# Re-spacing the substitution columns, the shared sums and the masks of a DeltaNet and hard-swish MLP kernel

## The chip, the cores and the metric

The kernel runs on one core of one Trainium2 chip. Its time is the device time of one execution in microseconds (us). Engines are named as in the profile: PE is TensorE (PEld its weight loads), DVE is VectorE, ACT is ScalarE, POOL is GpSimd, SP is SyncE. L756 is line 756 of the kernel before; in the kernel after, lines behind the first hunk stand one or two lower.

## The reference

A linear-attention recurrence (DeltaNet, with 4 batches, 8 heads, 768 tokens, head size 48) is followed by an MLP with a hard-swish (3072 tokens, 384 to 2048 to 384). All is fp32.

```python
k_n = k / (norm(k) + 1e-06)
for t in range(768):                     # state: (B, H, 48, 48)
    y[:, :, t] = einsum('bhd,bhde->bhe', q[:, :, t], state)
    v_old = einsum('bhde,bhd->bhe', state, kt)
    state = state + bt * einsum('bhd,bhe->bhde', kt, vt - v_old)
x = y.transpose(0, 2, 1, 3).reshape(3072, 384)
h = x @ w_in
out = (h * clip(h + 3, 0, 6) / 6) @ w_out
```

## The kernel before

**Chunks.** The recurrence is done in 24 chunks t of 32 tokens of all four batches (128 rows). Within a chunk the dependence of tokens on each other is a triangular system with a 32x32 matrix L for each batch and head. Its inverse X is found first, and then the chunk costs a few small matmuls. The names that matter:

- `prep(t)`: normalises k into `kb` (POOL, L502), makes the masks `mb` from beta (POOL, two operations of 128x256, L478), transposes k and q on PE (`pt`, L518), copies them to `KQ` (ACT), forms the scores `sc` (PE, L539) and multiplies them by `mb` into `L` and `LB` (DVE, L550), and at the end makes `bkb` (POOL, L490). `mb` has a single buffer, so a mask waits until L550 of the chunk before has read the last one.
- `inverse(g)`: the forward substitution for a group g of four chunks, 128 systems at once, on DVE: a transpose of L in (L461), 30 columns with two operations each (L751 multiplies into `pr`, L756 subtracts it from `A`; together 60 steps), a memset of the diagonal (L760) and a transpose out into `X` (L465). All four chunks of group g need this X. Groups 3 to 6 hold chunks 9 to 12, 13 to 16, 17 to 20 and 21 to 23.
- `chain(t)`: what goes from chunk to chunk. PE forms `ks` from the state (L798). DVE makes R in two halves: R1 is L892 (two operations), R2 is L898 (one). PE forms `pz` from X and R (L819), ACT copies it out, PE forms the state's update `su` (L927), and DVE subtracts it from `state` (L945). On its side the output: y from `ks` (ACT L835, DVE L811), plus `py` (PE L819, DVE L854, called y2 below), transposed on PE (`yt`, L864) into `xT` for the MLP.

**MLP.** Blocks of two chunks. `up` multiplies by w_in, `down` by w_out. From block 2 on `down_by_seven` does the down product as a 2x2 block scheme of seven products, with sums of g on DVE (L1197) and of the outputs on POOL and DVE (L1221). From block 5 on `up_by_eleven` does the up product in eleven block products for every pair of feature tiles j (0 to 7): `begin(j)` runs four matmuls, ACT copies the four quarters to `g` (L1069), POOL makes three sums of 128x128 that two products share (`plus_minus`, L1020), `end(j)` runs seven more matmuls into the same PSUM tile, and DVE adds the shared sums to it (L1085, L1086). The hard-swish follows on ACT (L1092, L1096) and DVE (L1099).

**Order.** The whole program is recorded by hand: each engine executes its instructions in the order in which the Python code emits them. The first chunks follow a written list (`ORDER`). From chunk 5 on, a loop emits every chunk as 15 units u = 0 to 14. In each unit it first takes the steps of chain and prep that `plan` sets for this u, then one unit of the MLP (one piece of `up`, `down` or their block forms, some 1.7 us of PE), then some steps of `fill`, which is the inverse of the next group for most of the time. For a chunk with i = t's place in its group: `ks` is emitted in u 0, R1 in u 1, R2 in u 2, `pz` in u 4, L550 in u 5, the update and y2 in u 8 to 10. The inverse of the next group is opened in u 6 of i = 1 (L461; for group 3 it is u 0 of i = 2). `left` counts the 62 takes that remain. In a unit

```python
room = max(1.65 - USED[mode["of"]] - CHAIN.get(u, 0), 0.15) / mode["mean"]
due += room * left / max((GS - i) * NU - u, 1)
due = min(due, 3.0)
take(fill, int(due))
left, due = max(left - int(due), 0), due - int(due)
```

`USED` is what DVE has to do for the MLP in such a unit, `CHAIN` what the chain asks of it in unit u, `mean` a mean of the room. In i = 0 two steps a unit are taken, and at u 2 of i = 0 `drain(fill)` emits all that is left, since `pz` in u 4 needs X. The drain stands behind R2 in that unit. Line `if i == 1 == ready[0] and 5 < u < 9: continue` leaves out the first units after the opening.

Of the kernel before, what the change touches and what calls it, by code (L numbers as in the profile page):

```python
# [15 lines left out]
ALU = mybir.AluOpType  # L16
# [30 lines left out]
def kernel(  # L47
# [21 lines left out]
    nc = tc.nc  # L69
# [3 lines left out]
    P = B * C  # L73
# [131 lines left out]
    for j, value in enumerate((1.0, -1.0)):  # L205
        m = mask2[:, j, :]
        for b in range(B):
            nc.gpsimd.memset(mask2[rows(b), j, :], value)
            nc.gpsimd.affine_select(
                out=mask2[rows(b), j, :], in_=mask2[rows(b), j, :], pattern=[[1, C]],  # L210
# [286 lines left out]
    def prep(t, whole=True):  # L497

        g, i = group(t)
        kb, qb = kbufs[t % NKB], qbufs[t % NQB]  # L500
        needs(*([("bkb", t - NKB)] if t >= NKB else []), *(pad(t) if t < NKB and t else []))
        nc.gpsimd.tensor_tensor(  # L502
            out=kb[:, :, 0:D], in0=kfs[g][:, i],
            in1=invs.pop(t).unsqueeze(2).to_broadcast([P, H, D]), op=ALU.mult,
        )
        past.add(("kb", t))
        if whole:
            drain(mask(t))
        yield

        for j, src in enumerate((kb, qb)):
            if j == 1:
                needs(("q", t))
                past.add(("qT", t))
            ring("pm", NPM, ("pt", t, j))
            pt = psM.tile([128, NP, P], FP32, name="pt", tag="pm")
            for p in range(NP):
                nc.tensor.transpose(  # L518
                    pt[:, p, :], src[:, 2 * p : 2 * p + 2].rearrange("p e w -> p (e w)"), ident[:]
                )  # L520
            yield 1
            if j == 0:
                ring("KQ", NKQ, ("KQ", t))
                KQ = work.tile([128, NP * B // 2, 4, C], FP32, name="KQ", bufs=NKQ)
            read(("pt", t, j))
            nc.scalar.activation(
                out=KQ[:, :, 0:4:3, :] if j == 0 else KQ[:, :, 1:3, :],
                in_=pt[:].rearrange("q p (x y c) -> q (p x) y c", y=2, c=C), func=ACTF.Copy,
            )
            yield  # L530
        ring("pc", NPC, ("sc", t))
        sc = psC.tile([P, 2, 512], FP32, name="sc", tag="pc")
        scv = sc[:, :, 0 : NP * 2 * C].rearrange("p e (a j w) -> p e a j w", a=NP, j=2)
        for p in range(NP):
            for b in range(B):
                for e in range(2):
                    r = slice(DP * e, DP * e + DP)
                    kq = KQ[r, p * B // 2 + b // 2]
                    nc.tensor.matmul(  # L539
                        scv[rows(b), e, p],  # L540
                        lhsT=kq[:, 3 if b % 2 else 0, :],
                        rhs=kq[:, 3:1:-1, :] if b % 2 else kq[:, 0:2, :],
                        start=True, stop=True,
                    )
        yield
        needs(*([("BZ", t - NLB)] if t >= NLB else []))
        LB = work.tile([P, H, C], FP32, name="LB", bufs=NLB)
        mb = mbs.pop(t)
        for j, out in enumerate((lowers(t), LB)):
            nc.vector.tensor_tensor(  # L550
                out=out.rearrange("p (e a) w -> p e a w", e=2), in0=scv[:, :, :, j, :],
                in1=mb[:, :, :, j, :], op=ALU.mult,
            )
        past.add(("L", t))
        KQs[t], LBs[t] = KQ, LB
        read(("sc", t), *([("KQ", 0)] if t == 0 else []))
        if whole:
            drain(scaled(t))
        yield
# [396 lines left out]
    mode = {"of": "down", "mean": 0.72}  # L956
# [51 lines left out]
    UF = 5  # L1008
# [10 lines left out]
    def plus_minus(out, a, b, op):  # L1019
        nc.gpsimd.tensor_tensor(out=out, in0=a, in1=b, op=op)  # L1020
# [28 lines left out]
    def up_by_eleven(blk):  # L1049
        needs(("sums", blk))  # L1050
        B11, T3x, B21, B22, B31, B32 = x_tiles(blk)
        phs, ready = {}, {}

        def mm(ph, n, w, x, start=False, stop=False):
            nc.tensor.matmul(  # L1055
                ph[:, n], lhsT=w, rhs=x, start=start, stop=stop, skip_group_check=True
            )

        def begin(j):
            key = ("ph", blk, "by", j)  # L1060
            ring("pm", NPM, key)
            ph = phs[j] = psM.tile([128, 4, P], FP32, name="ph", tag="pm")
            mm(ph, 0, W11[:, j], B11, start=True)
            mm(ph, 1, S1[:, j], T1x)
            mm(ph, 2, W21[:, j], T3x)
            mm(ph, 3, S2[:, j], T2x)
            gs[blk, j] = mlp.tile([128, 2, TB], FP32, name="g", bufs=NFC // 2)
            gt = gs[blk, j][:].rearrange("p i (t c) -> p (i t) c", c=P)
            nc.scalar.activation(out=gt, in_=ph[:], func=ACTF.Copy)  # L1069
            plus_minus(gt[:, 1], gt[:, 1], gt[:, 2], ALU.add)  # L1070
            plus_minus(gt[:, 2], gt[:, 0], gt[:, 1], ALU.add)
            plus_minus(gt[:, 0], gt[:, 0], gt[:, 3], ALU.add)

        def end(j):
            ph = phs.pop(j)
            mm(ph, 0, W12[:, j], B21)
            mm(ph, 1, S4[:, j], B22)
            mm(ph, 2, W22[:, j], T4x)
            mm(ph, 0, W13[:, j], B31)
            mm(ph, 1, W13[:, j], B32)  # L1080
            mm(ph, 2, W23[:, j], B31)
            mm(ph, 3, W23[:, j], B32, stop=True)
            g = gs[blk, j][:].rearrange("p i c -> p (i c)")
            gt = gs[blk, j][:].rearrange("p i (t c) -> p (i t) c", c=P)
            nc.vector.tensor_tensor(out=gt[:, 3], in0=ph[:, 3], in1=gt[:, 2], op=ALU.add)  # L1085
            nc.vector.tensor_tensor(  # L1086
                out=gt[:, 1:3], in0=ph[:, 1:3],
                in1=gt[:, 0].unsqueeze(1).to_broadcast([128, 2, P]), op=ALU.add,
            )

            def first():
                nc.scalar.activation(out=gt[:, 0], in_=ph[:, 0], func=ACTF.Copy)  # L1092
                read(("ph", blk, "by", j))
                ro = mlp.tile([128, CB, DM], FP32, name="o", bufs=1)
                r = ro[:].rearrange("p c m -> p (c m)")[:, 0 : 2 * TB]
                nc.scalar.activation(out=r, in_=g, func=ACTF.Relu, bias=half, scale=1.0 / 6.0)  # L1096

                def rest():
                    nc.vector.scalar_tensor_tensor(  # L1099
                        out=g, in0=r, scalar=1.0, in1=g, op0=ALU.min, op1=ALU.mult  # L1100
                    )

                ready[j] = rest

            ready[j] = first
            if j == NPR - 1:
                past.add(("up", blk))

        def go(j):
            if j in ready:  # L1110
                ready.pop(j)()

        begin(0)
        yield
        begin(1)
        yield
        for j in range(NPR):
            end(j)
            go(j - 1)
            if j + 2 < NPR:  # L1120
                yield
                begin(j + 2)
                go(j)
                yield
            else:
                go(j)
                if j == NPR - 1:
                    go(j)
                yield
# [148 lines left out]
    def mlp_units():  # L1278
# [20 lines left out]

        for blk in range(1, N // CB):  # L1300
            mode["of"] = "down"
            mode["mean"] = 0.72 if blk + 1 < UF else 0.45
            sums = weight_sums() if blk == UF - 1 else iter(())
            for _ in downs(blk):
                next(sums, None)
                next(sums, None)
                yield
            if blk + 1 < N // CB:
                mode["of"] = "eleven" if blk + 1 >= UF else "up"
                for n, _ in enumerate((up_by_eleven if blk + 1 >= UF else up)(blk + 1)):  # L1310
                    if blk + 1 == FIRST and n >= HF:
                        drain(rest)
                        if n % 2:
                            last_quarter(n - HF - 1)
                    yield
# [11 lines left out]
    def drain(gen):  # L1327
        for _ in gen:
            pass
# [87 lines left out]
    with tc.manual_schedule():  # L1417
# [11 lines left out]
        loads = iter(())  # L1429
        left = due = 0  # L1430
        USED = {"up": 0.42, "eleven": 1.0, "down": 0.8}
        CHAIN = {1: 0.75, 2: 0.75, 3: 0.4, 4: 0.4, 6: 0.8, 9: 0.8, 10: 0.8}
        for t in range(LS, N):
            g, i = group(t)
            ch = chain_of(t)
# [29 lines left out]
            for u in range(NU):  # L1465
# [15 lines left out]
                settle(1)  # L1481
                while evicts:
                    evicts.pop(0)()
                if i == 1 == ready[0] and 5 < u < 9:
                    continue
                if i == 0 or not left:
                    take(fill, 2 if i or u < 2 else u > 4)
                    continue
                room = max(1.65 - USED[mode["of"]] - CHAIN.get(u, 0), 0.15) / mode["mean"]
                due += room * left / max((GS - i) * NU - u, 1)  # L1490
                due = min(due, 3.0)
                take(fill, int(due))
                left, due = max(left - int(due), 0), due - int(due)
            drain(ch)
# [32 lines left out]
```

## Time and profile before

| | us |
|---|---|
| median of 3 runs | 680.05 |
| the three runs | 678.49, 680.05, 1275.28 |
| profiled execution | 677.9 |
| its span, first to last instruction | 676.2 |
| busy in it: PE / PEld / DVE / ACT / POOL | 638.2 / 579.8 / 500.0 / 272.3 / 221.1 |

The profiled execution's own time is 1.7 us longer than its span. In the profile's line of 40 slices, one slice is 16.9 us. Chunk 5, where the loop starts, begins at 160.5 us (its `ks`), and the last chunk (23) at 615.0 us, so a chunk is some 25 us long. A line of a group of instructions reads: source line, engine, operation, output and inputs, shape, count, then busy time and mean duration, then the idle time of the engine just before them and what ended it.

### The profile page before, as it was taken

The numbers are of one execution on the slowest core, as the hardware profiler recorded it, in microseconds if no ns is written. First come the engines' busy times: TensorE is split into PE (matmuls) and PEld (weight loads), VectorE is DVE, ScalarE is ACT, GpSimd is POOL, SyncE is SP. The second block draws the span as 40 slices with busy tenths as digits, with TensorE's granted clock in tenths as the row PEclk, the third lists the DMA queues.
The fourth block names the chain that finished last, engine by engine and source line by source line (L and its number), as shares of the span: only waits on it lengthen the run. The fifth ranks groups of instructions, "written<-read, shape, count | busy, mean of one in ns | idle before, by whom it ended". The sixth has DMA issues, their size and how long they took to land.

```text
span 676.2 us, 26940 instructions
## 1 busy us (share of the span) xinstructions
PE 638.2 (94%) x11768; PEld 579.8 (86%) x11768; DVE 500.0 (74%) x1226; ACT 272.3 (40%) x532; POOL 221.1 (33%) x376
## 2 busy tenths in 40 slices
PE   2568989999999999999999999999999999999997
PEld 2457977776689988988999999999999999999997
DVE  5998867888546699747888957998747998557264
ACT  5995767422143132232244244244244143143250
POOL 6230232002521121236165255065052151442340
PEclk9978989999999999999999999999999999999999
DMA  7896435402041030032030030020020020010000
GB/s 190 214 231 147 97 75 147 82 1 48 17 87 22 3 71 3 2 72 37 3 71 4 3 73 2 3 61 2 3 49 3 2 49 2 15 25 3 26 1 23
DMA packets 88501, 33.29 MB, mean 49 GB/s; under 512 B 80160, under 2 KB 83232, under 8 KB 88384
## 3 DMA queue, kind: packets, MB, share of 16 engines
q1 hardware_dynamic: 88128, 31.29, 20.4%
q8 instruction: 92, 1.51, 0.9%
q10 hardware_dynamic: 256, 0.30, 0.2%
q14 instruction: 25, 0.20, 0.1%
HBM read 26.84 MB, written 4.72 MB: 47 GB/s over the span
## 4 chain that ended last, share of the span: by engine, by line
PE 82%; DMA 6%; DVE 6%; issue 2%; ACT 1%; SPq 1%; POOL 1%; DVEq 0%; ACTq 0%; POOLq 0%
PE po L1211 27%; PE ph L1055 17%; PE ph L983 15%; PE po L1146 6%; PE ks L798 3%; DMA w_out<-in_moe_w_in_dram 3%; PE py L819 3%; PE pz L819 3%; PE su L927 3%; PE pt L518 2%; PE sc L539 2%; DMA qb<-in_q_dram 1%; PE yt L864 1%; DVE A L756 1%; DVE pr L751 1%
## 5 line engine op out<-in xcount | busy, mean ns | idle before, releaser
L1055 PE MATMUL ph<-xT,w_in 128*128 128x128 f32 x784 | 122.9, 278 | 0.0
L983 PE MATMUL ph<-xT,w_in 128*128 128x256 f32 (+1 forms) x576 | 117.0, 356 | 0.7 <-ACT spare L348 0.5
L1211 PE MATMUL po<-w_out,g 128*128 128x192 f32 x640 | 110.6, 326 | 0.0
L983 PEld LDWEIGHTS ph<-xT,w_in 128*128 128x128 f32 x576 | 96.3, 197 | 12.6 <-DVE g L994 0.6
L1055 PEld LDWEIGHTS ph<-xT,w_in 128*128 128x128 f32 x784 | 103.9, 192 | 1.3
L1020 POOL TENSOR_TENSOR g<-g 128x128 f32<-128x128 f32 x168 | 79.7, 476 | 75.4 <-ACT g L1069 66.2
L1211 PEld LDWEIGHTS po<-w_out,g 128*128 128x128 f32 x640 | 104.1, 190 | 0.2
L1211 PE MATMUL po<-spare,g 128*128 128x192 f32 x480 | 86.7, 332 | 0.0
L1211 PEld LDWEIGHTS po<-spare,g 128*128 128x128 f32 x480 | 77.2, 190 | 1.8
L1221 POOL TENSOR_TENSOR o<-o,u 128x192 f32<-128x192 f32 x18 | 18.6, 1035 | 167.2 <-ACT o L1218 93.5
L991 ACT ACTIVATE g<-ph,halves 128x256 f32<-128x256 f32 (+1 forms) x96 | 41.2, 437 | 78.3 <-PE ph L983 78.1
L1069 ACT ACTIVATE g<-ph 128x512 f32<-128x512 f32 x56 | 33.4, 597 | 80.5 <-PE ph L1055 77.0
L1197 DVE TENSOR_TENSOR g<-g 128x256 f32<-128x256 f32 x160 | 62.7, 440 | 3.5 <-PE po L1211 3.1
L756 DVE TENSOR_TENSOR A<-A,pr 128x30 f32<-128x30 f32 (+9 forms) x150 | 59.5, 397 | 3.6
L751 DVE TENSOR_TENSOR pr<-A 128x30 f32<-128x30 f32 (+9 forms) x150 | 56.1, 374 | 3.4
L994 DVE SCALAR_TENSOR_TENSOR g<-g,ph 128x256 f32<-128x256 f32 (+1 forms) x96 | 35.0, 371 | 25.2 <-ACT g L991 24.7
L348 ACT ACTIVATE spare<-spare,places 128x768 uint16<-128x768 uint16 (+1 forms) x56 | 52.5, 941 | 1.6 <-DMA spare<-in_moe_w_in_dram 0.6
L1099 DVE SCALAR_TENSOR_TENSOR g<-o,g 128x512 f32<-128x512 f32 x56 | 42.5, 759 | 6.6 <-ACT o L1096 6.6
L1218 ACT ACTIVATE o<-po 128x192 f32<-128x192 f32 x40 | 13.3, 331 | 80.5 <-PE po L1211 76.3
L1146 PE MATMUL po<-w_out,g 128*128 128x384 f32 x128 | 45.6, 493 | 0.0
L1096 ACT ACTIVATE o<-g,halves 128x512 f32<-128x512 f32 x56 | 40.5, 722 | 12.6 <-DVE g L1099 8.9
L478 POOL TENSOR_TENSOR mb<-beta_tok,mask 128x256 f32<-128x256 f32 x38 | 27.0, 730 | 55.8 <-DVE LB L550 55.8
(141 smaller groups left out, 985.2 us busy)
## 6 DMA issues: line engine op xcount, KB each, us to landing
kf<-in_k_dram SPq DMA_DIRECT2D x96, 48.0 KB, 2.8
qb<-in_q_dram SPq DMA_DIRECT2D x96, 48.0 KB, 2.8
vf<-in_v_dram SPq DMA_DIRECT2D x96, 48.0 KB, 2.1
out_dram<-o SPq DMA_DIRECT2D x92, 48.0 KB, 1.6
spare<-in_moe_w_in_dram SPq DMA_DIRECT2D x4, 768.0 KB, 7.7
w_out<-in_moe_w_in_dram SPq DMA_DIRECT2D x4, 768.0 KB, 8.0
w_out<-in_moe_w_out_dram SPq DMA_DIRECT2D x4, 768.0 KB, 5.6
spare<-in_moe_w_out_dram SPq DMA_DIRECT2D x4, 768.0 KB, 4.4
```

The lines of the kernel that those rows point to most:

```text
L348: nc.scalar.activation(out=z, in_=z if n else d.bitcast(I16)[:, :, :, 3], func=func, bias=places[:, n : n + 1], scale=scale,)
L751: nc.vector.tensor_tensor(out=pv, in0=A[:, j + 1 :, j].unsqueeze(2).to_broadcast([n, w, j]), in1=A[:, j, 0:j].unsqueeze(1).to_broadcast([n ...
L756: nc.vector.tensor_tensor(out=A[:, j + 1 :, 0:j], in0=A[:, j + 1 :, 0:j], in1=pv, op=ALU.subtract)
L819: nc.tensor.matmul(ps[rows(place(b)), D * h : D * h + D], lhsT=m(h)[rows(b)], rhs=z[rows(b), D * at(h) : D * at(h) + D], start=True, stop= ...
L983: nc.tensor.matmul(ph[:, cols], lhsT=w_in[:, s, f * 128 : (f + 1) * 128], rhs=xT[:, s, cols], start=(s == 0), stop=(s == NKT - 1),)
L991: nc.scalar.activation(out=g, in_=ph, func=ACTF.Relu, bias=half, scale=1.0 / 6.0)
L1020: nc.gpsimd.tensor_tensor(out=out, in0=a, in1=b, op=op)
L1055: nc.tensor.matmul(ph[:, n], lhsT=w, rhs=x, start=start, stop=stop, skip_group_check=True)
L1099: nc.vector.scalar_tensor_tensor(out=g, in0=r, scalar=1.0, in1=g, op0=ALU.min, op1=ALU.mult)
L1146: nc.tensor.matmul(pos[c][:], lhsT=gs[blk, f // 2][:, f % 2, c * P : (c + 1) * P], rhs=w_out[:, f, :], start=(f == 0), stop=(f == NFC - 1),)
L1197: nc.vector.tensor_tensor(out=A(f, *out), in0=A(f, *a), in1=A(f, *b), op=op)
L1211: nc.tensor.matmul(ps[n][:], lhsT=A(f - f % 2, *a)[:, f % 2], rhs=b[:, f], start=(f == 0), stop=(f == HF - 1),)
```

## The change

Five edits.

1. In `prep`, the mask is emitted one step later: not directly after `kb` but after the first transposes and their copy.
2. In `up_by_eleven`, the three shared sums become two POOL operations. The first takes both 128x128 sums in one operation whose first and output operands run over the quarters backwards (`3:1:-1`), and what the two DVE operations of `end` add is renamed to match; the larger one (two quarters) now stands first.
3. Columns start in u 7 of i = 1 instead of u 9 (`5 < u < 7`).
4. `due` is held at 2.6, so at most two steps a unit are taken instead of three.
5. `CHAIN` gets entries for u 0 and u 14 and smaller ones for u 6 and u 10; `mean` for blocks from 4 on is 0.4 instead of 0.45.

```diff
@@ prep
         past.add(("kb", t))
-        if whole:
-            drain(mask(t))
         yield
...
                 in_=pt[:].rearrange("q p (x y c) -> q (p x) y c", y=2, c=C), func=ACTF.Copy,
             )
+            if whole and j == 0:
+                drain(mask(t))
             yield
@@ up_by_eleven, begin
-            plus_minus(gt[:, 1], gt[:, 1], gt[:, 2], ALU.add)
-            plus_minus(gt[:, 2], gt[:, 0], gt[:, 1], ALU.add)
-            plus_minus(gt[:, 0], gt[:, 0], gt[:, 3], ALU.add)
+            plus_minus(gt[:, 3:1:-1], gt[:, 0:2], gt[:, 3:1:-1], ALU.add)
+            plus_minus(gt[:, 0], gt[:, 0], gt[:, 2], ALU.add)
@@ up_by_eleven, end
-            nc.vector.tensor_tensor(out=gt[:, 3], in0=ph[:, 3], in1=gt[:, 2], op=ALU.add)
             nc.vector.tensor_tensor(
                 out=gt[:, 1:3], in0=ph[:, 1:3],
-                in1=gt[:, 0].unsqueeze(1).to_broadcast([128, 2, P]), op=ALU.add,
+                in1=gt[:, 3].unsqueeze(1).to_broadcast([128, 2, P]), op=ALU.add,
             )
+            nc.vector.tensor_tensor(out=gt[:, 3], in0=ph[:, 3], in1=gt[:, 0], op=ALU.add)
@@ mlp_units
-            mode["mean"] = 0.72 if blk + 1 < UF else 0.45
+            mode["mean"] = 0.72 if blk + 1 < UF else 0.4
@@ the loop
-        CHAIN = {1: 0.75, 2: 0.75, 3: 0.4, 4: 0.4, 6: 0.8, 9: 0.8, 10: 0.8}
+        CHAIN = {0: 0.45, 1: 0.75, 2: 0.75, 3: 0.4, 4: 0.4, 6: 0.5, 9: 0.8, 10: 0.6, 14: 0.2}
...
-                if i == 1 == ready[0] and 5 < u < 9:
+                if i == 1 == ready[0] and 5 < u < 7:
                     continue
...
-                due = min(due, 3.0)
+                due = min(due, 2.6)
```

## The prediction, made before the changed kernel ran

> **What bounds the kernel now.** I read the page's engine lines and slices first, then the waits of PE from 200 us on, then a table of windows cut at the `ks` of the chunks, then timelines of DVE and PE at the places that had lost time.
>
> ```profile
> span 676.2 us, 26940 instructions
> PE 638.2 (94%) x11768; PEld 579.8 (86%) x11768; DVE 500.0 (74%) x1226; ACT 272.3 (40%) x532; POOL 221.1 (33%) x376
> PE   2568989999999999999999999999999999999997
> PEld 2457977776689988988999999999999999999997
> PEclk9978989999999999999999999999999999999999
> ...
> PE pz L819 <- DVE R L898: 1.8, 3, 0.8
> PE py L819 <- issue: 0.5, 1, 0.5
> PE pz L819 <- ACT o L1218: 0.4, 1, 0.4
> PE yt L864 <- DVE y L854: 0.4, 1, 0.4
> PE ph L983 <- DVE g L994: 0.2, 1, 0.2
> ```
>
> PE is full from the ninth slice on, at full clock. The five waits are all that it had from 200 us to the end: 3.3 us. The rest of its 38 us of idle time is in the opening, which `ORDER` writes, and at the very end; no edit reaches either. The windows of chunks 8, 12, 15, 16 and 20 (length, PE, PEld, DVE, ACT, POOL busy) say where:
>
> ```profile
> 240.90:267.10 26.20, 25.97 (x426) 22.02 (x425) 24.78 (x70) 9.14 (x19) 2.77 (x4) 1.00 0.19 36
> 343.40:369.50 26.10, 25.40 (x495) 24.44 (x495) 22.97 (x52) 12.47 (x25) 16.84 (x30) 1.00 0.20 41
> 419.70:445.40 25.70, 25.26 (x459) 24.15 (x458) 23.57 (x66) 6.50 (x14) 5.42 (x9) 1.00 0.04 10
> 445.40:471.90 26.50, 25.30 (x495) 24.37 (x495) 24.27 (x53) 12.56 (x25) 16.97 (x30) 1.00 0.17 33
> 544.00:568.20 24.20, 23.37 (x424) 22.73 (x422) 21.42 (x54) 12.09 (x25) 10.37 (x22) 1.00 0.13 28
> ```
>
> Length less PE: 0.23, 0.70, 0.44, 1.20 and 0.83 us, 3.4 in all; DVE is over 88% busy in each. Chunk 16 shows how it comes about (four lines of DVE's timeline, then one of PE's; start, duration, engine, line):
>
> ```profile
> 449.81 0.53 DVE L756 TENSOR_TENSOR A<-A,pr 128x220 f32<-128x220 f32 x1
> 450.37 0.52 DVE L751 TENSOR_TENSOR pr<-A 128x210 f32<-128x210 f32 x1
> 450.81 0.73 DVE L892 SCALAR_TENSOR_TENSOR R<-ks,parity,vf 128x192 f32<-128x192 f32 x2
> ...
> 452.89 0.60 DVE L898 SCALAR_TENSOR_TENSOR R<-ks,parity,R 128x384 f32<-128x384 f32 x1
> 453.64 0.88 PE L819 MATMUL pz<-R,X 32*32 32x48 f32 x64 [0.83 <-DVE R L898]
> ```
>
> Columns stand without a gap ahead of R1; R2 ends at 453.49 and `pz` starts 0.15 us later, after 0.83 us of idle PE. So PE sets the time and DVE's lateness at R2 is the only thing to win.
>
> **What the Trainium skill says.** "Perfetto Trace Analysis", Identifying the Most-Contended Engine: matmul busy time misleads, the weight loads' share is the better sign. The trace agrees with PE as bound: PEld is 22.7 to 24.4 us in the last four windows. "SBUF — State Buffer", Who interferes with whom: a DVE operation with two SBUF inputs and a GpSimd one that reads SBUF exclude each other. The trace fits: the subtraction of 128x108 took 0.27 us at 423.13, with POOL idle, and 0.68 at 367.62, while POOL made a mask. "GPSIMD Engine Reference", Elementwise — side-by-side cycle accounting: a fixed part plus 2.6 cycles an element at 1.2 GHz, 2.2 ns. Here 128 elements took 476 ns (168 of L1020) and 256 took 728 (L1020 on w_in): 1.97 ns an element, 224 ns fixed. Performance pitfalls for Q7 kernels, in the same page: an inner step over 8 bytes costs half as much again. Here only the outer step is reversed and the inner stays 4 bytes, so I charge nothing.
>
> **The change part by part.** I counted the DVE instructions in the built order of both kernels. PE, ACT and SP have the same instructions in the same order; only DVE's and POOL's orders differ. So PE's work is unchanged and the sum is over waits.
>
> *Columns, gains.* Steps ahead of R2, counted from the last point at which DVE had been idle, before and after:
> - Chunk 8: 16 to 12. At 0.40 us a step R2 and the L994 behind R1 come 1.6 us sooner; the 0.23 goes.
> - Chunk 12: 12 to 9, at 0.5: 1.5 us sooner; 0.2 goes. The other 0.5 in this chunk is the wait in `py` for "issue", which nothing here touches: it stays.
> - Chunk 15: 12 to 8, the four smallest (0.21 to 0.27): 0.96 us sooner; 0.44 goes.
> - Chunks 16 and 20: 12 to 9 each, at 0.53: 1.6 us sooner against 0.83 lost; both go.
> - Chunk 16, `yt` behind y2 (0.37): eight steps to seven larger ones since DVE's last idle point at 458, 3.28 to about 3.0 us: 0.3 goes.
>
> Sum 0.23 + 0.2 + 0.44 + 0.83 + 0.83 + 0.3 = 2.8 us.
>
> *Columns, losses.* With two a unit the substitution ends later.
> - Chunk 9: all 60 steps and the transpose stood ahead of R1. Now two steps stand in each of u 0 and u 1 and the drain behind R2 holds six steps, the memset and the transpose. R2 then ends near 271.7. Six small steps (1.45 us from start to start, as at 265 to 266.7), 0.12 and 1.98 give X at 275.2, so `pz`, which ran at 274.77, starts at 275.3: 0.6 us lost. If POOL ran beside them (0.3 more a step) it would be 2.4 more; POOL then waited for ACT until 275.3, so I take 0.6.
> - Chunks 13, 17 and 21: memset and transpose move to u 0, still ahead of R1. Two, three and three more steps stand behind the last L1099 (0.55 to 0.85 us) and one fewer ahead of it (0.6). Chunk 13: 0; chunk 17: 0.2; chunk 21 has 0.8 us of slack between R2 and `pz`: 0.
> - Chunk 14: four small steps, 0.94 us, now stand ahead of y2, whose slack to `yt` is 0.97: 0, with no cover left; chunks 10 and 18 have 2.0 and 1.5.
>
> Sum 0.8.
>
> *Two operations for three.* 3 x 476 = 1.43 us becomes 728 + 476 = 1.20, 56 times: 13 us less POOL. POOL is idle 75 us ahead of L1020, so that is hidden; DVE's wait for POOL (14.7 us, seven waits) shortens, but those lie where R2 has slack. Bounds: if the reversed operand cost as two, nothing is won; if it cost twice 728, a j takes 1.9 us of the 3.4 that its two units last, still hidden. I take 0.
>
> *Masks.* A mask waits less at the head of POOL's queue (32.3 us in three waits), with the weight sums of block 4 and other sums behind it. It is needed at L550, three or four units (5 to 7 us) after its new place and lasts 1.2 to 1.7 us. Hidden; 0 either way, to 0.5 lost if a mask fell behind a waiting L1221.
>
> Total: -2.8 + 0.8 = -2.0 us. The profiled execution would go from 677.9 (span 676.2 and 1.7 around it) to 675.9. The median shown, 680.05, is 2.15 above that execution, and the lowest run 678.49; the mean of these three is 678.8, so I predict 676.8.
>
> **Rivals.** *The gain is eaten (no change in sum).* Each stall that goes uncovers the next: y2 in chunks 12 and 20 has 0.45 us to `yt`, chunk 15 0.28. PE arrives earlier, DVE has the same total work. Half of the 2.8 stays and 0.8 to 1.5 is lost: about 678.5. For it: DVE over 88% in those windows. Against: fewer or equal steps stand ahead of y2 there too. *Slower: X comes late.* One mechanism, the substitution's end crowded against `pz` in chunks 9, 13, 17 and 21. If POOL runs beside it, 8 to 10 steps gain 0.3 us each in chunk 9 (3.0 lost), and 1.0 each in the others: 6 us lost, 2.8 won, about 682. It decides once X's transpose ends past 274.6 by more than 3 us in chunk 9. Against: POOL idle there. *The change does not do what it says:* it does; u 1 and u 2 emit 0 or 1 step as before, and what thins R is the cap and u 0, so this is no case of its own.
>
> **Numbers.** Forecast (stalls go, 676.8) 0.62, own range 674.5 to 678; eaten 0.23; late X 0.12; something that I do not see 0.03. Range 673.5 to 681.5: below, all 3.4 us won and run-to-run scatter of 2 us; above, most of late X. Two per cent, 13.6 us, is about what a measurement of this kernel can tell from no change: PE has only 3.4 us to give back, so faster by that 0.01, slower 0.03, within 0.96.
>
> **What would show it.** Right: no wait of `pz` for L898 in chunks 12, 16 and 20, none of L983 in chunk 8, PE busy within 1 us of 638; a wait of `pz` for L465 near 275 us of 0.3 to 1 us; L1020 with 112 operations and some 67 us. Wrong: new waits of `pz` or `yt` over 1 us, `pz` waiting for X after chunk 9, or L550 waiting for POOL's masks.

## The result, and the profile after

The kernel after takes 676.67 us (median of 20 runs, 674.59 to 680.25) where the kernel before takes 680.64 (median of 20 of its runs on the same chip; a stray one at 1275 us is left out of the comparison). The ratio of the runs is 0.9952 [0.9936, 0.9968], or 3.3 us less (2.2 to 4.4); the two medians alone differ by 4.0. The forecast was 676.8. The profiled execution took 675.37 us, against 677.9 before.

The page after, lines of the span, of the engines and of PE's slices, then the largest POOL group:

```profile
span 673.6 us, 26871 instructions
PE 636.8 (95%) x11768; PEld 578.6 (86%) x11768; DVE 497.2 (74%) x1226; ACT 271.2 (40%) x532; POOL 206.4 (31%) x320
...
PE   2667989999999999999999999999999999999997
...
L1020 POOL TENSOR_TENSOR g<-g 128x256 f32<-128x256 f32 x112 | 68.1, 610 | 83.9 <-ACT g L1069 79.5
```

PE has the same 11768 matmuls and is full in the same slices. The waits of PE from 160 us to the end, by what ended them (total us, times, longest):

```profile
PE pz L819 <- DVE R L898: 0.6, 1, 0.6
PE pz L819 <- DVE X L465: 0.3, 1, 0.3
```

Two waits of 0.9 us stand where five of 3.3 us stood: all five of before are gone, and the two that are left stand in chunks 9 and 18. The five windows of before, cut again at the `ks` of chunks 8, 12, 15, 16 and 20:

```profile
241.80:267.40 25.60, 25.60 (x427) 22.26 (x425) 22.48 (x60) 9.09 (x19) 2.92 (x4) 1.00 0.20 37
343.70:368.70 25.00, 25.00 (x496) 24.31 (x495) 22.57 (x52) 12.46 (x25) 14.90 (x23) 1.00 0.22 43
418.90:444.00 25.10, 25.10 (x458) 24.03 (x457) 23.03 (x62) 6.38 (x14) 5.34 (x8) 1.00 0.04 9
444.00:469.30 25.30, 25.30 (x497) 24.33 (x496) 22.17 (x51) 12.46 (x25) 15.01 (x23) 1.00 0.18 35
542.10:565.40 23.30, 23.30 (x424) 22.70 (x423) 20.52 (x50) 11.98 (x25) 8.78 (x15) 1.00 0.14 29
```

PE is busy over the whole length of each, while each is 0.6 to 1.2 us shorter. Chunk 16, shown in the prediction, is the clearest (DVE's timeline; start, duration, engine, line; in brackets the idle time before it and its releaser):

```profile
447.39 0.74 DVE L892 SCALAR_TENSOR_TENSOR R<-ks,parity,vf 128x192 f32<-128x192 f32 x2
448.90 0.42 DVE L1084 TENSOR_TENSOR g<-ph,g 128x256 f32<-128x256 f32 x1 [0.77 <-PE ph L1055]
...
450.36 0.60 DVE L898 SCALAR_TENSOR_TENSOR R<-ks,parity,R 128x384 f32<-128x384 f32 x1
451.84 0.88 PE L819 MATMUL pz<-R,X 32*32 32x48 f32 x64
```

The last line is PE's: `pz` now starts without a wait, 0.88 us after R2 has ended (before: 0.15 us), and DVE even stands idle for 0.77 us between R1 and R2.

**A finer measure.** Ends of matmuls in the trace are modelled, so part of a stall shows as wider spacing rather than as idle time: in chunk 8 the windows of before show 0.23 us of idle PE, but the chunk became 0.68 us shorter. Since PE has the same instructions in the same order in both kernels, I measure a chunk from its first `ks` matmul to the next chunk's first. Where neither an edit nor a late output transfer (below) reaches, these lengths repeat within 0.04 us. Worked out from the traces of before, after and a second execution of the kernel after (`after_again`, below):

```
chunk        8     9     12     13    15     16    17    18    20    5 to end
before     26.22 25.59  26.12  25.23 25.63  26.53 25.24 23.34 24.23   515.2
after      -0.68 +0.39  -1.09  -0.11 -0.51  -1.20 -0.09 +0.71 -0.89   -3.4
after_again-0.68 +0.38  -1.08  -0.12 -0.52  -1.19 -0.11  0    -0.89   -4.2
```

All others differ by 0.04 us or less. The opening, ahead of chunk 5, took 160.7 to 164.9 us over all profiled executions without any edit reaching it (161.0 before, 161.8 after). So the trace says -4.2 us when chunk 18 behaves, and the spread of the opening hides part of that in the time of a whole execution.

**A length can move without an edit.** The hard-swish on ACT (L1095; L1096 before) writes into the buffer `o`, which the last output transfers of a block still read. In chunks 12 and 16 its first operation starts 3.07 us after `ks`, or 0.30 us after the last of these transfers has landed, whichever is later. This holds within 0.02 us in 27 of the 28 places in the fourteen traces; in the other, chunk 16 of `sums_only`, it started later still. ACT's copy into `KQ` (L524) stands directly behind it, so PE's waits of `ph` for KQ below are mostly this wait, passed on. No edit is needed to move the landing. From chunk 10 on, `fix9` (below) has the same instructions in the same order on each engine as the kernel after. Yet in its chunk 16 the transfer landed 3.62 us after `ks` instead of 3.10, the hard-swish came 0.52 us later, and the chunk was 0.52 us longer. First chunk 16 of the kernel after and of `fix9`, then chunk 12 of `columns_only`, where the landing was at 3.50 us instead of 2.74:

```profile
447.93 0.72 ACT L1095 ACTIVATE o<-g,halves 128x512 f32<-128x512 f32 x1 [0.36 <-ACT g L1091]
448.10 0.72 ACT L1095 ACTIVATE o<-g,halves 128x512 f32<-128x512 f32 x1 [0.88 <-DMA out_dram<-o]
```

```profile
347.38 0.73 ACT L1096 ACTIVATE o<-g,halves 128x512 f32<-128x512 f32 x1 [0.76 <-DMA out_dram<-o]
```

The first line names ACT, but L1091 had ended 0.36 us before. So each length of chunks 12 and 16 below has to be read together with the start of this hard-swish in the same trace.

### The profile page after: what moved, and what is told of

The parts are those of the page before. It is cut to its first block, busy times and chain, and to the rows that moved or that the text cites. A ratio compares the mean times of both kernels' runs of the same rounds, so it can differ in the third digit from the quotient of the medians.

```text
span 673.6 us, 26871 instructions
## 1 busy us (share of the span) xinstructions
PE 636.8 (95%) x11768; PEld 578.6 (86%) x11768; DVE 497.2 (74%) x1226; ACT 271.2 (40%) x532; POOL 206.4 (31%) x320
## 4 chain that ended last, share of the span: by engine, by line
PE 86%; DVE 6%; DMA 2%; ACT 2%; issue 2%; SPq 1%; POOL 0%; ACTq 0%; DVEq 0%; POOLq 0%
PE po L1210 27%; PE ph L1055 20%; PE ph L983 15%; PE po L1145 6%; PE ks L798 3%; PE pz L819 3%; PE su L927 3%; PE py L819 3%; PE sc L539 3%; PE pt L516 3%; ACT spare L348 1%; PE yt L864 1%; DVE spare L375 1%; DMA spare<-in_moe_w_in_dram 1%; DMA qb<-in_q_dram 1%
## 5 line engine op out<-in xcount | busy, mean ns | idle before, releaser
L983 PE MATMUL ph<-xT,w_in 128*128 128x256 f32 (+1 forms) x576 | 114.9, 350 | 3.4 <-DVE g L994 2.1
L983 PEld LDWEIGHTS ph<-xT,w_in 128*128 128x128 f32 x576 | 94.3, 192 | 15.3 <-DVE g L994 2.5
L1055 PEld LDWEIGHTS ph<-xT,w_in 128*128 128x128 f32 x784 | 103.9, 192 | 1.4 <-ACT KQ L524 0.2
L1020 POOL TENSOR_TENSOR g<-g 128x256 f32<-128x256 f32 x112 | 68.1, 610 | 83.9 <-ACT g L1069 79.5
L1220 POOL TENSOR_TENSOR o<-o,u 128x192 f32<-128x192 f32 x18 | 15.0, 835 | 172.1 <-ACT o L1217 97.4
L994 DVE SCALAR_TENSOR_TENSOR g<-g,ph 128x256 f32<-128x256 f32 (+1 forms) x96 | 35.0, 370 | 26.0 <-ACT g L991 25.7
L1084 DVE TENSOR_TENSOR g<-ph,g 128x256 f32<-128x256 f32 x56 | 23.4, 419 | 38.1 <-PE ph L1055 24.1
L1098 DVE SCALAR_TENSOR_TENSOR g<-o,g 128x512 f32<-128x512 f32 x56 | 40.8, 729 | 7.3 <-ACT o L1095 7.3
L1095 ACT ACTIVATE o<-g,halves 128x512 f32<-128x512 f32 x56 | 40.5, 722 | 11.3 <-DVE g L1098 5.7
```

The costliest lines, as they stand in the source:

```text
L983: nc.tensor.matmul(ph[:, cols], lhsT=w_in[:, s, f * 128 : (f + 1) * 128], rhs=xT[:, s, cols], start=(s == 0), stop=(s == NKT - 1),)
L1055: nc.tensor.matmul(ph[:, n], lhsT=w, rhs=x, start=start, stop=stop, skip_group_check=True)
L1098: nc.vector.scalar_tensor_tensor(out=g, in0=r, scalar=1.0, in1=g, op0=ALU.min, op1=ALU.mult)
```

## The experiments

The theory: DVE's lateness at R and at y2 is all there is to win, and the columns' edits (3, 4, 5) alone win it; edits 1 and 2 are worth nothing. Its rivals: the two-for-three sums or the masks pay; or the gain hangs on one of the three column edits and the others are idle.

**Again, and one edit group at a time.** `after_again` is the kernel after, unaltered:

> The changed kernel once more, unaltered, to see what of its trace repeats. Theory (stalls): PE's idle time from chunk 5 on is again 0.3 to 1.2 us, with pz waiting for X in chunk 9 by 0.3 to 0.6 us; the wait of pz in chunk 18 (0.6 us, behind an ACT operation that waited for an output DMA) and the absence of the 0.55 us gap inside py of chunk 12 may differ from execution to execution. Rival (POOL): the same. Time 0.993 to 0.997 of the kernel before.

Measured: 0.9965 [0.9947, 0.9983]. Its only wait of PE is that of `pz` for X; the one of 0.6 us for R2 (chunk 18) is not there.

`columns_only` is before with edits 3 to 5:

```diff
-            mode["mean"] = 0.72 if blk + 1 < UF else 0.45
+            mode["mean"] = 0.72 if blk + 1 < UF else 0.4
-        CHAIN = {1: 0.75, 2: 0.75, 3: 0.4, 4: 0.4, 6: 0.8, 9: 0.8, 10: 0.8}
+        CHAIN = {0: 0.45, 1: 0.75, 2: 0.75, 3: 0.4, 4: 0.4, 6: 0.5, 9: 0.8, 10: 0.6, 14: 0.2}
-                if i == 1 == ready[0] and 5 < u < 9:
+                if i == 1 == ready[0] and 5 < u < 7:
-                due = min(due, 3.0)
+                due = min(due, 2.6)
```

> Edits 3 to 5 alone: start of the columns, cap of two, weights and mean; masks and three POOL sums as before. Theory (stalls at R2): nearly the whole gain, 2.5 to 3.5 us, ratio 0.9955; the waits of pz for L898 in chunks 12, 15, 16 and 20 and of L983 in chunk 8 are gone, pz waits for X in chunk 9 by 0.4 us. Rival (POOL: DVE gets faster because POOL takes the shared reads less often): under 1 us, ratio 0.999, and the waits of pz stay.

Measured: 0.9966 [0.9952, 0.998]; chunk 5 to the end -2.5 us. Waits of PE:

```profile
PE ph L1055 <- ACT KQ L526: 0.4, 1, 0.4
PE pz L819 <- DVE X L465: 0.3, 1, 0.3
PE yt L864 <- DVE y L854: 0.3, 1, 0.3
PE pz L819 <- DVE R L898: 0.2, 1, 0.2
```

The columns win most of it, but 1.6 us of -4.2 are missing, nearly all in chunks 12 (-0.31 for -1.08) and 16 (-0.61 for -1.19) and in chunk 17 (+0.18 for -0.11). Timing alone could not have told the two apart; the lengths do. But in chunk 12 the hard-swish started 0.73 us later than in `after_again`, which leaves next to nothing of the 0.77 there to the edits, and in chunk 16 0.15 us later. With these two taken out the columns come to about -3.4 us, by this estimate from the traces. What is left, 0.43 us in chunk 16 (`yt` waits for y2) and 0.29 in chunk 17 (`pz` waits for R2), belongs to the other edits.

`sums_only` is before with edit 2:

```diff
-            plus_minus(gt[:, 1], gt[:, 1], gt[:, 2], ALU.add)
-            plus_minus(gt[:, 2], gt[:, 0], gt[:, 1], ALU.add)
-            plus_minus(gt[:, 0], gt[:, 0], gt[:, 3], ALU.add)
+            plus_minus(gt[:, 3:1:-1], gt[:, 0:2], gt[:, 3:1:-1], ALU.add)
+            plus_minus(gt[:, 0], gt[:, 0], gt[:, 2], ALU.add)
```

> Edit 2 alone: the shared sums in two POOL operations, columns and masks as before. Theory (stalls at R2): 0 to 0.6 us gained, ratio 0.9995; L1020 takes 68 us instead of 80, the waits of pz in chunks 15, 16 and 20 stay above 0.3 us each. Rival (POOL): 2 us or more, ratio 0.997, with those waits gone since the columns beside POOL run faster.

Measured: 1.0031 [1.0015, 1.0047], slower; chunk 5 to the end +2.1 us (chunk 12 +0.88, 16 +0.67, 18 +0.58, 20 +0.42, 15 -0.26). The 0.58 of chunk 18 is a late output transfer (last section), so some 1.5 us are left to the edit. The largest waits of PE:

```profile
PE pz L819 <- DVE R L898: 4.1, 5, 1.2
PE yt L864 <- DVE y L854: 1.1, 2, 0.5
```

With 13 us less POOL work, DVE became later at R2. That was not in any of my cases; the last experiment takes it up.

`mask_only` is before with edit 1:

```diff
-        if whole:
-            drain(mask(t))
         yield
...
+            if whole and j == 0:
+                drain(mask(t))
             yield
```

> Edit 1 alone: masks one step later. Theory (stalls at R2): 0, within 0.3 us, ratio 1.000; waits of pz as before. Rival (POOL): 1 us gained, because the mask no longer stands beside the columns ahead of R1 in chunks 12, 16 and 20.

Measured: 1.0004 [0.9987, 1.002]; chunk 5 to the end -0.1 us. Alone the masks are worth nothing that these runs can tell.

**One edit taken back from the kernel after.** `sums_undone` has the three sums of before, all else as after:

> The changed kernel with three POOL sums again (columns and masks as changed). From the start of chunk 5 to the end the changed kernel took 511.8 and 511.1 us, the kernel before 515.2, columns alone 512.7, sums alone 517.3. Theory 1 (a 256-wide POOL sum holds up a column longer than a 128-wide one, which costs only where R2 has no slack): with the columns thinned the sums are worth nothing or a little, so 511 to 512.5 us, ratio to before 0.993 to 0.998. Theory 2 (two sums are a loss of 2 us anywhere): 509 to 510 us, ratio 0.991 to 0.993. Theory 3 (two sums only pay together with the columns): 512.7 us or more, ratio 0.997.

Measured: 0.9962 [0.9944, 0.9979]; -2.7 us by the lengths, 1.5 less than `after_again`: chunk 12 -0.63 instead of -1.08, chunk 16 -0.45 instead of -1.19, chunk 17 +0.17 instead of -0.11. Of these, 0.40 in chunk 12 and 0.32 in chunk 16 are a later start of the hard-swish behind an output transfer. What is left is 0.42 in chunk 16 and 0.28 in chunk 17, the same as in `columns_only`. So the same edit that costs some 1.5 us alone earns some 0.7 us when the columns are thinned.

`mask_undone` has the mask in its old place:

> The changed kernel with the mask directly after kb again (columns and sums as changed). Theory 1 (the mask's place hides): 511 to 512 us from chunk 5 on, ratio 0.9955. Theory 2 (it matters that the mask no longer stands ahead of the sums of chunks 12, 16 and 20): 0.5 to 1.5 us longer, waits of pz for L898 or of ph for L524 there, ratio 0.998.

Measured: 0.9936 [0.9915, 0.9957]; -3.7 us by the lengths, 0.5 less than `after_again`: 0.24 in each of chunks 12 and 16 and nothing elsewhere. But in these two chunks the hard-swish started 0.33 and 0.24 us later, behind a later output transfer, which leaves nothing to the masks; nothing shows that the masks move the transfers. In time this run is the shortest of all. By steps, with the output transfers taken out: columns about -3.4, sums on top of them about -0.7, masks 0; together -4.1 of the -4.2.

The three column edits, each taken back alone. `weights_undone`:

```diff
-            mode["mean"] = 0.72 if blk + 1 < UF else 0.4
+            mode["mean"] = 0.72 if blk + 1 < UF else 0.45
-        CHAIN = {0: 0.45, 1: 0.75, 2: 0.75, 3: 0.4, 4: 0.4, 6: 0.5, 9: 0.8, 10: 0.6, 14: 0.2}
+        CHAIN = {1: 0.75, 2: 0.75, 3: 0.4, 4: 0.4, 6: 0.8, 9: 0.8, 10: 0.8}
```

> The changed kernel with the old weights of the chain and the old mean (cap of two and the start in u 7 as changed). Steps ahead of R2 since DVE's last wait go from 9 to 11 in chunks 12, 16 and 20, from 7 to 9 in chunk 13 and from 8 to 9 in chunks 15, 17 and 21; 12 as before the change. Theory (stalls at R2, less the slack there): 0.5 + 0.3 + 0.8 in chunks 12, 16 and 20, 0.2 to 0.3 each in 13, 17 and 21: 2 us more than the changed kernel, ratio to before 0.998. Rival (the cap and the start did it): within 0.5 us of the changed kernel, ratio 0.996.

Measured: 0.9961 [0.9944, 0.9977]; -2.8 us, which is 1.3 less than `after_again` where 2 were expected. Against it, chunks 13, 17 and 21 lost 0.48, 0.48 and 0.28 us. There X's transpose now stands behind R1 on DVE, and R2 behind the transpose: in chunk 13 R2 ends 7.68 us after `ks` (6.88 in the kernel after), and `pz` starts 0.15 us later. Chunk 12 lost 0.11 us and chunk 16 0.29, of which 0.23 is a late output transfer. Chunk 9 won back its 0.39.

`cap_undone`:

```diff
-                due = min(due, 2.6)
+                due = min(due, 3.0)
```

> The changed kernel with up to three steps a unit again (start in u 7, weights and mean as changed). Steps ahead of R2 since DVE's last wait: 16 in chunk 8 (12 with the cap), 10 in chunks 12, 16 and 20 (9), 10 in chunk 15 (8), 3 or 4 in chunks 13, 17 and 21 (7 or 8). Theory: the wait of L983 in chunk 8 (0.23 us) comes back, the one of chunk 9 (0.31) goes, chunks 16 and 20 stay free or lose up to 0.3: within 0.6 us of the changed kernel, 511 to 512 us from chunk 5 on, ratio 0.995 to 0.997. Rival (the cap is the main edit): 1.5 us or more longer.

Measured: 0.9997 [0.9978, 1.0016]; -0.8 us by the lengths. The expectation was wrong. Waits of PE:

```profile
PE ph L983 <- DVE g L994: 1.1, 1, 1.1
PE yt L864 <- DVE y L854: 0.7, 2, 0.5
PE ph L1055 <- ACT KQ L524: 0.4, 1, 0.4
```

Chunk 8 has 16 steps ahead of R2 again, and PE waits 1.1 us for the L994 behind R1. Five of the steps last 0.65 to 0.89 us beside POOL's work instead of 0.40, but so they do before; why the chunk is 0.85 us longer than before is open. Chunks 15 and 16 give back nearly all that they had won (-0.08 and -0.09 against before). In chunk 16 `yt` waits 0.5 us, and 0.45 us is a late output transfer, as 0.32 us is in chunk 12. That leaves some 2.6 us to the cap.

`start_undone`:

```diff
-                if i == 1 == ready[0] and 5 < u < 7:
+                if i == 1 == ready[0] and 5 < u < 9:
```

> The changed kernel with the columns starting in u 9 again (cap, weights and mean as changed). The substitution then ends later: 10 steps stand behind DVE's last wait in chunks 13, 17 and 21 (7 or 8), 10 in chunks 12, 16 and 20 (9), and in chunks 18 and 22 nothing but a last piece is drained. Theory (X's and R2's lateness): 0.5 us in chunk 13, 0.6 in 17, 0.4 in 21, 0.1 to 0.3 in 12, 16 and 20: 1.5 to 2 us more than the changed kernel, 513 to 513.5 us, ratio 0.998. Rival (the start is worth nothing): within 0.4 us.

Measured: 1.002 [1.0004, 1.0035]; +0.7 us by the lengths, of which 0.7 is chunk 18 and 0.44 a gap in `py` (both below). Without these two it is 3.7 us more than `after_again`, where 1.5 to 2 were expected. Waits of PE, then, from the timelines of DVE and PE, `pz` of chunk 17 with the transpose ahead of it:

```profile
PE pz L819 <- DVE X L465: 2.2, 3, 1.0
PE pz L819 <- DVE R L898: 1.3, 2, 0.6
PE yt L864 <- DVE y L854: 0.6, 1, 0.6
PE py L819 <- issue: 0.4, 1, 0.4
```

```profile
478.86 1.94 DVE L465 STREAM_TRANSPOSE X<-A 128x1024 f32<-128x1024 f32 x1
480.95 0.88 PE L819 MATMUL pz<-R,X 32*32 32x48 f32 x64 [0.98 <-DVE X L465]
```

This is the prediction's rival "X comes late", in chunks 17 and 21 (0.93 us each): with the cap at two a unit and no earlier start, the substitution does not end in time. In chunk 13 R2, behind X's transpose, is late by 0.6 us. So the cap and the start belong together: the cap thins R, the start pays for it. With either taken back little of the gain is left; neither was run alone.

**What R2's lateness costs.** `delay` is the kernel after with two DVE operations of 128x384 more ahead of R2:

```diff
+            if t >= 7:
+                for _ in range(2):
+                    nc.vector.tensor_tensor(out=R, in0=R, in1=R, op=ALU.max)
```

> The changed kernel with two extra DVE operations (the maximum of R with itself, 128x384, nothing computed by them) directly ahead of R2 in every chunk from 7 on, some 0.9 to 1.0 us together. Theory (R2's lateness passes one to one into PE where its slack is used up): by the slack between R2's end and pz in the changed kernel (less 0.15 us), chunks 7 to 11, 19 and 23 absorb it, 15 and 16 lose 0.1 to 0.3, 12 and 14 0.5, 13 0.7, 20 to 22 0.8 each, 17 and 18 1.0 each: 6 to 6.5 us more than the changed kernel, ratio to before 1.004 to 1.006. Rival (PE is full, R2 has little to do with it): under 1.5 us more, ratio below 0.998.

Measured: 1.0145 [1.0121, 1.0169]; +9.3 us by the lengths against before, +13.5 against `after_again`. The added group from the view of the tile R (shortest, median and longest of 34 in ns, first and last start), then PE's two largest waits:

```profile
L900 DVE TENSOR_TENSOR R<-R x34: 542/557/1081, 222.4 to 631.4; 128x384 f32<-128x384 f32 x34
```

```profile
PE pz L819 <- DVE R L901: 9.7, 9, 2.5
PE pz L819 <- DVE X L465: 1.4, 1, 1.4
```

Two operations are 1.1 us. Chunks 9, 13, 17 and 21 became longer by 1.14, 0.88, 1.19 and 1.01 us against `after_again`: about one to one, so these have no slack left. Chunks 14, 20 and 22 lost 1.2 to 1.5 us. Chunk 12 (0.70) and chunk 18 (2.56) have a late output transfer as well. My expectation, 6 to 6.5 us, was half of what was measured: it took 0.9 to 1.0 us for the two operations, counted slack in chunk 9, and left out that X's transpose in chunk 9 stands behind R2. What it shows is that R2 is the right place: in these four chunks 1 us there is 1 us of time, in chunk 9 by way of X.

**The new wait in chunk 9.** `fix9` puts eight steps instead of two into u 0 of chunk 9:

```diff
-                    take(fill, 2 if i or u < 2 else u > 4)
+                    take(fill, 8 if (t, u) == (9, 0) else 2 if i or u < 2 else u > 4)
```

> The changed kernel, but in u 0 of chunk 9 eight steps of the substitution are taken instead of two, so that only the last column, the memset and the transpose are left for the drain behind R2. Theory: DVE was idle for 0.7 us ahead of R1 and 0.4 us at L1196 there, so X comes 0.5 to 1 us sooner and the wait of pz for L465 in chunk 9 (0.31 us in every trace with the cap) is gone, with R2 of chunk 9 still over 2 us early: 0.3 us less than the changed kernel from chunk 5 on, 510.8 to 511.5 us, ratio 0.995. Rival (the transpose itself, 2 us, is what is late): the wait stays at 0.2 us or more.

The same two instructions in the kernel after, then in `fix9`:

```profile
273.24 1.98 DVE L465 STREAM_TRANSPOSE X<-A 128x1024 f32<-128x1024 f32 x1
275.37 0.88 PE L819 MATMUL pz<-R,X 32*32 32x48 f32 x64 [0.31 <-DVE X L465]
```

```profile
272.11 1.98 DVE L465 STREAM_TRANSPOSE X<-A 128x1024 f32<-128x1024 f32 x1
275.01 0.88 PE L819 MATMUL pz<-R,X 32*32 32x48 f32 x64
```

The transpose comes 1.13 us sooner, the wait is gone and chunk 9 is back to its length of before (0.00). In time, 0.9969 [0.9952, 0.9986] can't be told from the kernel after: 0.38 us is worth 0.0006, and this execution had the wait of chunk 18 (0.80 us) and the late transfer of chunk 16 (0.52).

**Why the same sums cost or earn.** If the sums' POOL time mattered, more of it would be worse; if it is how long one POOL operation holds a DVE step up, shorter operations would be better though POOL works longer (120.6 us from 200 us on, in 336 operations of 368 ns, against 80 in 168 of 476). `sums_halved` is before with each of the three sums cut into two of 64:

```diff
+            for c in (slice(0, P // 2), slice(P // 2, P)):
-            plus_minus(gt[:, 1], gt[:, 1], gt[:, 2], ALU.add)
-            plus_minus(gt[:, 2], gt[:, 0], gt[:, 1], ALU.add)
-            plus_minus(gt[:, 0], gt[:, 0], gt[:, 3], ALU.add)
+                plus_minus(gt[:, 1, c], gt[:, 1, c], gt[:, 2, c], ALU.add)
+                plus_minus(gt[:, 2, c], gt[:, 0, c], gt[:, 1, c], ALU.add)
+                plus_minus(gt[:, 0, c], gt[:, 0, c], gt[:, 3, c], ALU.add)
```

> The kernel before with each of the three shared sums split into two operations of 64 columns, six of some 350 ns for three of 476 (2.1 us of POOL for 1.43 a pair of tiles). Theory 1 (a column beside a POOL operation waits for that operation to end, so the longest operation decides): the extra time of a column beside these sums falls from 130 ns on average and 263 at most to 60 to 100 and at most 150 to 200. Theory 2 (columns slow down by POOL's share of the time): it grows with POOL's busy time, to 150 ns or more, and the waits of pz in chunks 15, 16 and 20 grow. Time to before 0.999 to 1.003.

Measured: 0.9996 [0.9979, 1.0013]; -0.5 us by the lengths, but with columns as before chunks 12, 15, 16 and 20 became shorter by 0.22, 0.50, 0.47 and 0.81 us. Chunks 18 (+0.95) and 23 (+0.71) gave most of it back: the output wait below, and `po` behind L1100. In chunk 16, `sums_only` first (two lines of DVE's timeline, two of POOL's), then `sums_halved` (two steps of DVE, one line of POOL):

```profile
448.39 0.82 DVE L756 TENSOR_TENSOR A<-A,pr 128x240 f32<-128x240 f32 x1
453.77 0.80 DVE L751 TENSOR_TENSOR pr<-A 128x220 f32<-128x220 f32 x1
...
448.17 1.36 POOL L1020 TENSOR_TENSOR g<-g 128x256 f32<-128x256 f32 x2 [0.96 <-ACT g L1069]
451.91 2.98 POOL L1020 TENSOR_TENSOR g<-g 128x256 f32<-128x256 f32 x4
```

```profile
445.19 0.41 DVE L756 TENSOR_TENSOR A<-A,pr 128x240 f32<-128x240 f32 x1
445.63 0.41 DVE L751 TENSOR_TENSOR pr<-A 128x238 f32<-128x238 f32 x1
...
444.96 2.58 POOL L1020 TENSOR_TENSOR g<-g 128x64 f32<-128x64 f32 x6 [0.95 <-ACT g L1069]
```

All four steps begin while POOL makes sums. Beside the long ones the two last 0.82 and 0.80 us, twice their least (0.40 and 0.38); beside the short ones the two last their least. The last 12 steps ahead of R1 of chunk 16 are the same in before, `sums_only` and `sums_halved`; their durations sum to 6.71, 7.11 and 5.37 us. The chunk's length is 26.53, 27.20 and 26.07.

The same for all steps from 200 us on, the time of a step above the least of its form, by what POOL did beside it (counts in brackets): nothing 5 ns (164); sums of 128 wide, before, mean 130 and at most 263 ns (40); both sums of a pair, 256 and 128 wide, `sums_only`, mean 371 and at most 537 ns (18); sums of 64 wide, `sums_halved`, mean 32, where 60 to 100 was expected, and at most 133 ns (56). "SBUF — State Buffer", Who interferes with whom, in the Trainium skill, says that such operations exclude each other; these runs agree, and add that the hold grows with the length of the one POOL operation (368 ns for the 64 wide, 476 for the 128, 754 for the 256). Over all columns the extra is 16.2 us before, 19.2 in `sums_only`, 12.4 in `sums_undone` and 15.3 in the kernel after.

This explains the loss alone: in chunk 16 R2 ends 0.48 us later in `sums_only` than before, and 0.40 of it are these steps.

The gain beside thinned columns comes from another DVE operation, the hard-swish L1099 (L1098 with two sums), which reads two tensors too. It stands beside `kb` or `bkb`, which POOL takes up directly behind the sums. Two sums are done sooner than three, so the operation behind them is done sooner too. Ahead of R1 of chunk 17, first `sums_undone`, then the kernel after:

```profile
468.79 1.29 DVE L1099 SCALAR_TENSOR_TENSOR g<-o,g 128x512 f32<-128x512 f32 x1
468.70 0.83 POOL L502 TENSOR_TENSOR kb<-kf,inv 128x384 f32<-128x384 f32 x1
```

```profile
466.54 1.03 DVE L1098 SCALAR_TENSOR_TENSOR g<-o,g 128x512 f32<-128x512 f32 x1
466.20 0.83 POOL L502 TENSOR_TENSOR kb<-kf,inv 128x384 f32<-128x384 f32 x1
```

In both the hard-swish ends 0.54 to 0.55 us after `kb` (470.08 after 469.53, 467.57 after 467.03), so what it loses is the rest of POOL's operation. That is 0.26 us less with two sums, and chunk 17 is 0.28 us shorter. In chunk 16 the same happens beside `bkb` (1.24 and 0.97 us), and a step right ahead of y2 takes 0.62 us beside a sum and 0.32 us otherwise. From the end of L550 to the end of y2 it takes 7.37 us in `columns_only` and `sums_undone`, but 6.94 or 6.95 in the kernel after, `after_again`, `mask_undone` and `fix9`: the 0.42 us of chunk 16. Over the 56 operations of the hard-swish, the time above the least is 4.0 to 5.0 us in the four traces with three sums of 128, and 2.2 to 3.0 in the nine with two. So two sums hold the steps up more and the hard-swish less, and what counts is which of them stands where DVE has no slack.

## Why the prediction was right, and where its steps were off

- *PE's work unchanged, the sum is over waits:* shown. All five waits of before are gone, the matmuls are the same. PE's busy time fell by 1.4 us, where I had given it 1 us; stalls that hide in modelled ends would show so.
- *Chunk 8, 0.23:* right in cause, 0.68 in size. Its term was read from idle PE in a window, which shows a third of the stall. `cap_undone` puts the 16 steps and the wait for L994 back.
- *Chunk 15, 0.44; chunk 16, 0.83 + 0.3; chunk 20, 0.83:* 0.51, 1.20 and 0.89. Right, except for the 0.3 of `yt` in chunk 16: with the columns alone `yt` still waits 0.29 us, and only the two sums take that away.
- *Chunk 12, 0.2, the "issue" gap of 0.5 stays:* wrong. The chunk won 1.09, and the gap was gone. That the columns alone won only 0.31 is the late output transfer (0.73). A gap of this kind appears in one other trace (`start_undone`, chunk 16). It is gone in `mask_only` too, whose columns are those of before; there `yt` waits 0.36 us and the chunk is only 0.14 us shorter. So I can't say how much of the 1.09 is the gap. What makes it is open. Both gaps end 2.62 us after a packet of queue q8, which the page calls `instruction`, began; in chunk 12 of the other thirteen traces the same matmul comes at least 3.09 us after one. That would fit a PE that waits for its next instructions, but no run tests it.
- *Chunk 9, 0.6 lost:* the wait is there, at the place and with the releaser named (X at 275.22, `pz` at 275.37, predicted 275.2 and 275.3). That the times agree so closely is luck: `ks` of this chunk came 0.22 us later than before, since the opening was longer. From `ks`, X ends after 7.59 us, where the prediction's times give 7.8, and so the wait costs 0.39. `fix9` shows that it is the six steps behind R2.
- *Chunks 13 and 21: 0, chunk 17: 0.2 lost:* chunks 13 and 17 won 0.1 each, 21 nothing. That they hang on X, or on R2 behind X's transpose, is shown by `start_undone` and `weights_undone`, where they lose up to 1.0 against `after_again`.
- *Two for three, 0:* the step that failed. It is some +1.5 us alone and some -0.7 us beside the thinned columns. I asked only whether POOL's time was hidden, and overlooked that DVE's operations pay for the POOL operation beside them, though the prediction had quoted the very exclusion. The prices of 476 and 728 ns are means, and the first has such holds in it: the medians are 457 and 726, which is 2.1 ns an element and not 1.97.
- *Masks, 0, to 0.5 lost:* 0 alone, and 0 beside the rest once the output transfers are taken out.
- *Rivals.* "Eaten" did not happen: no wait moved to y2. "X late" happened at 0.3 us and once, in chunk 9; with the earlier start taken back it appears in chunks 17 and 21 too, which is where the prediction put it.

Sum: forecast -2.0 us from chunk 5 on, measured -3.4 and -4.2. The time, 676.67, fell nearer to the forecast than the lengths did, because I set the forecast to 676.8 from a mean of 678.8 for the kernel before, whose median over 20 runs is 680.64; the two errors, a gain too small and a base too low, are of opposite sign, so a miss of 0.1 us is luck. Nor is two per cent what a measurement of this kernel can tell: the interval above is 0.32% wide.

## What to carry to other kernels

Where one engine sets the time and another is late only at a few places, sum the waits at these places, but measure a stage from a fixed instruction to the next stage's: idle time between modelled ends showed a third of one stall. Before a difference of a few tenths is given to an edit, look in both traces for a wait that is there without it, as the one for the output transfers here. Price a GpSimd edit by what stands on VectorE beside it, not only by whether GpSimd's own time is hidden: the same two sums cost some 1.5 us beside dense columns and earned some 0.7 beside thin ones. Where work is spread over time slots, a lower cap and an earlier start belong together: without either one little of the gain was left.

## What the runs showed of the hardware that I had not expected

A reversed outer step costs POOL nothing visible: the 256-wide sum with reversed operands took 754 ns on average in the kernel after, against 728 for the forward one of before; the medians are 730 and 726.

Then chunk 18, which is 0.7 us longer in the kernel after and not in `after_again`. In the kernel after, ACT and SP's queue, then the same of `after_again`:

```profile
499.79 0.72 ACT L1095 ACTIVATE o<-g,halves 128x512 f32<-128x512 f32 x1 [1.74 <-DMA out_dram<-o]
492.03 4.92 SPq L1134 DMA_DIRECT2D out_dram<-o  x8
```

```profile
498.57 0.72 ACT L1095 ACTIVATE o<-g,halves 128x512 f32<-128x512 f32 x1
492.53 3.60 SPq L1134 DMA_DIRECT2D out_dram<-o  x8
```

SP took 4.92 us to issue the eight output transfers instead of 3.60, the last landed 4.67 us after `ks` instead of 1.83, and ACT waited 1.74 us for it, since the hard-swish writes into the buffer `o` that the transfer reads. The chain then leads to L1098, R2 and `pz`. It appears in six of the fourteen profiled executions (after, `sums_only`, `start_undone`, `fix9`, `delay`, `sums_halved`), once with and once without in the same kernel, so no edit makes it. In chunk 12 of `columns_only` and `delay` the last of the eight was issued late in the same way, 1.9 us after `ks` instead of 0.2. What holds SP up is open, and no run tried a second buffer there.
